# A spectral filter feeding a SiLU layer: table order, stand-ins and the places of weight rounding

## The chip, the cores and the metric

One core of a Trainium2 chip runs the kernel. The metric is the device time of one execution in microseconds (us); the median of several runs counts. Engines are called by their usual names: TensorE (PE) multiplies, PEld is its weight load, VectorE (DVE) and ScalarE (ACT) work element by element, GpSimd (POOL) does the same more slowly, and SyncE (SP) only issues transfers. An engine works through its instructions in order. ScalarE, SyncE and GpSimd also issue transfers (DMA); these rows carry a q, as in SPq.

## The reference

A Fourier filter along the sequence, then a two-layer product with SiLU between, all in float32:

```python
batch, seq, dim = 8, 3008, 256
X = np.fft.rfft(x, axis=1)
Y = X * (filt_r + 1j * filt_i)[None]
y = np.fft.irfft(Y, n=seq, axis=1).astype(np.float32)
x = y.reshape(24064, 256)
h = x @ w_in                          # 256 x 2048
g = h * (1.0 / (1.0 + np.exp(-h)))
out = (g @ w_out).astype(np.float32)  # 2048 x 256
```

## The kernel before

**Two jobs woven together.** The sequence length is 94 x 32. For each batch the spectral part does a first transform over 94 (tiles `pa`), stores and reloads, a second transform over 32 (`pb`), multiplies by the filter, does the two inverse transforms (`pc`, then `pd`, with a store to `d2` and a reload between) and evicts the result as `y`. The layer part takes pairs of 256 tokens from `y` and runs eight steps for a pair, one for each pair of 128-wide slices of the hidden dimension. Products of 2 x 2 blocks are formed from seven products instead of eight: a step has seven products into `px` and `pyz` in `hidden(step)` (L981) and the seven products of the step before into four accumulators in `project` (L1049). Before them, `tokens(pair)` forms the token combinations `ty`, and `combine_weights(jp)` forms the four weight combinations.

**Step and round.** A step is issued in eight rounds. In round 0 stands the first product into `px` and its copy (L989); in round 1 the product into `zo` (half of `pyz`) and its sum `g0`, then `finish()` (two subtractions for the step before); in round 2 the second product into `px` and its copy (L996); in round 3 a product into `yo`; in round 4 the third product into `px`, its copy (L1002) and the second sum of `pyz`; in round 6 the last product into `px`, which a silu then reads; in round 7 the last product into `yo`, whose sum `g1` is the last reader of `pyz`. `px` and `pyz` have one buffer each, so that the next step's products wait for these readers. `pending` is a list, sorted by step and round, of everything else that is to be issued; `put(step, rnd, piece, ...)` adds to it and `until(time)` issues what is due. The order of steps starts with three steps of pair 0, then eight of pair 1, then the rest of pair 0. Slices j = 2 jp and 2 jp + 1 of the weights must be ready when a step first uses jp: steps 0 to 2 use jp 0 to 2, and steps 3 to 10 use jp 0 to 7.

**Weights.** The weights arrive in 64 bits a number, and the kernel makes 32-bit numbers of them with integer and float operations: `load_weights(j)` loads a slice (512 KB), then `bits` (two operations on VectorE, L1179 and L1181), `converted` (two on ScalarE, L1188 and L1189), `added` (VectorE, L1195), `signed` (VectorE, L1200), `placed` (VectorE, L1207). `rounded` is `added` and `signed` in one call. A combination is four operations on VectorE (L952, w_t<-w_t).

**The start.** Batch 0 has nothing to hide behind, and its spectral part runs first, in the same places of `w_t` that the weights take later. `idle(n)` runs n products of no use on TensorE (stand-ins). `load_first` loads x in four parts of 768 KB; `stage1_first(j)` multiplies part j by the table wx3 (48 product records for two parts, since a float32 product is recorded twice) into four banks, and VectorE transposes them. Eight banks serve in turn, so part 2 reuses the banks of part 0. After the second transform of the first groups (`forward`, with twelve stand-ins ahead of group 0) come products, `inverse_first`, and `rows_first`, whose stores to `d2` go out on ScalarE's queue, the last two of the second halves on SyncE's. `load_t4_rows(k)` reloads the rows of groups 2k and 2k+1 (two transfers); `stage3(g)` is the last inverse transform of batch 0's first half. Weights 0 to 5 are begun before the steps. In steps 1 to 6, `stage1(u)` of batch 1 adds two products of 512 columns (L418) in round 3.

In the lists below, `(7, 1, (rounded, 12), ...)` means step 7, round 1.

Of the kernel before, what the change touches and what calls it, by code (L numbers as in the profile page):

```python
# [264 lines left out]
def kernel(  # L265
# [9 lines left out]
    nc = tc.nc  # L275
# [42 lines left out]
    wx_t = cpool.tile([96, 128], FP32)  # L318
# [24 lines left out]
    def bank(b, name, spare=None):  # L343


        if early[0] is None and spare in ("x", "yz"):
            return xps.tile([128, 2, C], FP32, name=name, tag=spare)
        if early[0] is None and spare is not None:
            return accps.tile([128, 2, C], FP32, name=name, tag=f"a{spare}")
        if early[0] is None:  # L350
            return fps.tile([128, 2, C], FP32, name=name, tag="f")
        early[0] += 1
        k = early[0] % 8
        if k < 2:
            return fps.tile([128, 2, C], FP32, name=name, tag="f")
        if k > 5:
            return xps.tile([128, 2, C], FP32, name=name, tag="x" if k == 6 else "yz")
        return accps.tile([128, 2, C], FP32, name=name, tag=f"a{k - 2}")

    def spectral(b):  # L360
# [21 lines left out]
            us["t4"] = view[:, 8960:13056].rearrange("p (n c) -> p n c", c=C)  # L382
            return view

        def stage1_first(j, fill=0):

            raw = [bank(b, f"pa_{b}_{j}_{q}") for q in range(4)]
            ps = [r.rearrange("p a c -> p (a c)").rearrange("p (n c) -> p n c", c=16) for r in raw]
            for _ in range(fill):
                nc.tensor.matmul(out=raw[0][:, 0, 0:128], lhsT=wx_t, rhs=wx_t, start=True, stop=True)  # L390
            for k in range(3):
                for q in range(4):
                    rows = slice(32 * q, 32 * q + 32)
                    nc.tensor.matmul(out=ps[q], lhsT=wx3_t[rows, k], rhs=xs[j][rows, k],  # L394
                                     start=(k == 0), stop=(k == 2), skip_group_check=True)
# [816 lines left out]
    def combine_weights(jp, part=None, eng=None):  # L1212

        eng = eng or v

        def w(c):
            first, by = {A12: (2, 3), S3: (4, -1)}.get(c, (2 * c, 1))
            return flat_w[:, jp, first:first + 2 * by:by]
        if part != 1:
            combine(eng, w(S1), w(S3), w(A22), ALU.add)  # L1220
            combine(eng, w(S2), w(S1), w(A11), ALU.subtract)
        if part != 0:
            combine(eng, w(S3), w(A11), w(S3), ALU.subtract)
            combine(eng, w(S4), w(A12), w(S2), ALU.subtract)
# [6 lines left out]
    def bits(*js):  # L1231
        if wide:
            bits_of_weights(*js)
# [22 lines left out]
    def placed(*js):  # L1256
# [4 lines left out]
                load_exact(j)  # L1261


    nc.scalar.dma_start(out=wx_t, in_=wx_dram.ap())
    wx3_t = qpool.tile([128, 2, C], FP32, name="wx3", tag="q").rearrange("p a c -> p (a c)")[:, 0:384].rearrange(
        "p (k m) -> p k m", k=3)
    nc.scalar.dma_start(out=wx3_t, in_=wx3_dram.ap())
    for i, value in enumerate((1151.0, 255.0 * (1 << 23))):
        nc.gpsimd.memset(bias_t[:, i:i + 1], value)
    for j in range(4):  # L1270
        for i in range(2):
            nc.gpsimd.memset(bias_t[32 * j:32 * j + 32, 3 + i:4 + i], 1.0 if j % 2 == i else -1.0)

    def idle(n, operand=None):

        ps = bank(0, "idle").rearrange("p a c -> p (a c)")
        rows = wx_t if operand is None else operand
        for _ in range(n):
            nc.tensor.matmul(out=ps[:, 0:128], lhsT=rows, rhs=rows, start=True, stop=True)

# [7 lines left out]
    wide_rows = d_t[0:96].rearrange("p s r n -> p (s r n)")[:, 0:256]  # L1288
    blank = x_all[0:96, 0, 0, 0:128]
    v.memset(blank, 0.0)  # L1290
    idle(14, operand=blank)

    part, second = spectral(0), spectral(1)
    part["load_first"]()
    nc.sync.dma_start(out=d_t[:, 0:16], in_=d_dram[:, 0:16])
    nc.sync.dma_start(out=f_all[:, :, 0:4], in_=filt_a)
    nc.sync.dma_start(out=e_t[:, 0:2], in_=e_dram[:, 0:2])
# [12 lines left out]
                                 scale=bias_t[:, 3:4])  # L1310

    for j in range(4):
        part["stage1_first"](j, 5 * (j > 1))
    second["load_two"]()
    weights(4, 5)
    part["forward"](0, fill=12)
# [26 lines left out]
    for k in range(2):  # L1343
        part["add"](NG - 1, k)
    part["load_t4_rows"](0)
    bits(0, 1)
    inverse(4)
    inverse(5)
    converted(0, 1)
    added(0, 1)  # L1350
    part["load_t4_rows"](1)
    part["load_t4_rows"](2)
    bits(2, 3)
    converted(2, 3)
# [4 lines left out]
    combine_weights(0)  # L1359
    rounded(2, 3)  # L1360
    placed(2, 3)
    combine_weights(1)
    bits(4, 5)
    converted(4, 5)
    added(4, 5)
    idle(20)
    for g in range(4):
        part["stage3"](g)
    gp.tensor_copy(out=gate, in_=y[0, 0][:, 0, 28:29])
# [14 lines left out]
    for b in range(1, B):  # L1384
        plan(b, second if b == 1 else spectral(b))
    for step, rnd, *todo in (
            (0, 1, (signed, 4), (placed, 4), (signed, 5)), (0, 5, (placed, 5), (bits, 6), (added, 6)),
            (1, 0, (converted, 6), (weights, 8, 9, 10)), (1, 1, (combine_weights, 2)), (1, 5, (signed, 6), (placed, 6)),
            (2, 1, (bits, 7), (added, 7)), (2, 2, (converted, 7), (weights, 11)),
            (2, 5, (bits, 8), (signed, 7), (placed, 7)), (3, 0, (converted, 8)),  # L1390
            (3, 1, (added, 8), (signed, 8), (placed, 8)), (3, 2, (weights, 12)), (3, 5, (bits, 9), (added, 9)),
            (4, 0, (converted, 9)), (4, 1, (bits, 10), (signed, 9), (placed, 9)),
            (4, 2, (converted, 10), (weights, 13)), (4, 5, (added, 10), (signed, 10), (placed, 10)),
            (5, 1, (combine_weights, 3), (bits, 11)), (5, 2, (converted, 11), (weights, 14, 15)),
            (5, 5, (added, 11), (signed, 11), (placed, 11)),
            (6, 1, (combine_weights, 4), (bits, 12)), (6, 2, (converted, 12)),
            (6, 5, (added, 12), (signed, 12), (placed, 12)),
            (7, 1, (combine_weights, 5), (bits, 13)), (7, 2, (converted, 13)),
            (7, 5, (added, 13), (signed, 13), (placed, 13)),
            (8, 1, (combine_weights, 6), (bits, 14)), (8, 2, (converted, 14)),  # L1400
            (8, 5, (added, 14), (signed, 14), (placed, 14), (bits, 15)), (9, 0, (converted, 15)),
            (9, 1, (added, 15), (signed, 15), (placed, 15)), (9, 5, (combine_weights, 7))):
        for piece, *args in todo:
            put(step, rnd, piece, *args)

# [78 lines left out]
```

## Time and profile before

| | us |
|---|---|
| median of 3 runs | 2517.6 |
| runs | 2517.13, 2517.6, 2519.85 |
| the profiled execution | 2519.81 |
| its span in the profile | 2518.0 |

| engine | busy us | share of the span |
|---|---|---|
| PE | 2491.2 | 99% |
| PEld | 2128.8 | 85% |
| DVE | 1759.4 | 70% |
| ACT | 1096.6 | 44% |
| POOL | 431.5 | 17% |

Times in the profile count from the start of the span. A row of the timeline has start, duration, engine, line, operation, tiles written and read, shapes and count; in brackets stands how long the engine was idle before it and what ended that. A row of the windows has the window, its length, then the busy time and number of instructions of PE, PEld, DVE, ACT and POOL, the granted clock of TensorE (1.00 is full), the share of time that the transfer engines were busy, and GB/s. A row of the waits has engine and line, what it waited for, the sum, how often, and the longest. A row of groups has the count, then busy us, mean ns of one, and idle time before. The line numbers are those of the kernel before; the changed kernel's differ by up to 5 from L388 on (its L392 is L394 here, its L979 is L981).

### The profile page before, as it was taken

The page shows a single profiled execution, that of the slowest core. Times are in us where ns is not written, and L with a number is a line of the kernel's source. Part 1 is how long each engine was busy: PE and PEld are TensorE (multiplying, and loading weights), DVE is VectorE, ACT ScalarE, POOL GpSimd, SP SyncE. Part 2 cuts the span into 40 slices and gives each one's busy share as a digit, 9 for nine tenths or more (in the row PEclk, how much of TensorE's full clock was granted, in tenths as well). Part 3 has the DMA queues.
Part 4 walks back from the last instruction along what each step waited for, and adds up shares of the span by engine and source line. Part 5 has one row for each costly group of instructions (what it writes and reads, how often), then busy time and mean ns, then how long its engine had stood idle before and what let it go on. Part 6 is the DMA issues. An engine that isn't in the chain of part 4 may idle for free.

```text
span 2518.0 us, 42288 instructions
## 1 busy us (share of the span) xinstructions
PE 2491.2 (99%) x16242; PEld 2128.8 (85%) x16242; DVE 1759.4 (70%) x3608; ACT 1096.6 (44%) x3006; POOL 431.5 (17%) x673
## 2 busy tenths in 40 slices
PE   9899999999999999999999999999999999999999
PEld 6678888888888888888888888888888888888988
DVE  6766677777777777777777777777677766655544
ACT  2544444444444444444444444444444444444443
POOL 2201221122121121211222111211122112101100
PEclk9999999999999999999999999999999999999999
DMA  7532141312322132320324203331042211200000
GB/s 268 168 77 88 54 119 46 93 51 58 81 68 72 49 80 60 88 76 25 93 49 117 62 23 79 82 78 43 26 102 66 55 43 34 63 21 9 17 9 17
DMA packets 140089, 170.67 MB, mean 68 GB/s; under 512 B 20892, under 2 KB 113404, under 8 KB 139260
## 3 DMA queue, kind: packets, MB, share of 16 engines
q1 hardware_dynamic: 115824, 120.77, 18.3%
q0 software_dynamic: 22080, 44.10, 6.8%
q8 instruction: 127, 2.08, 0.3%
q10 hardware_dynamic: 1984, 3.11, 0.3%
q14 instruction: 74, 0.61, 0.1%
HBM read 96.06 MB, written 81.26 MB: 70 GB/s over the span
## 4 chain that ended last, share of the span: by engine, by line
PE 96%; DVE 3%; ACT 1%; DMA 0%; issue 0%; POOL 0%; DVEq 0%
PE acc L1049 45%; PE px L981 25%; PE pyz L981 19%; PE pd L756 1%; PE pf L488 1%; PE pc L584 1%; PE pb L546 1%; DVE g L952 1%; PE pa L394 1%; PE pc L662 0%; PE pb L528 0%; PE pa L418 0%; DVE w_t L1207 0%; DMA wx<-wx_tbl 0%; DVE w_t L952 0%
## 5 line engine op out<-in xcount | busy, mean ns | idle before, releaser
L1049 PE MATMUL acc<-g,w_t 128*128 128x256 f32 (+1 forms) x5376 | 1507.7, 376 | 3.0 <-ACT o L769 2.5
L1049 PEld LDWEIGHTS acc<-g,w_t 128*128 128x128 f32 x5376 | 1016.1, 190 | 154.4 <-ACT o L769 15.3
L952 DVE TENSOR_TENSOR g<-pyz,abc 128x256 f32<-128x256 f32 (+1 forms) x1152 | 479.7, 416 | 483.7 <-ACT abc L1002 246.8
L952 DVE TENSOR_TENSOR g<-g 128x256 f32<-128x256 f32 (+3 forms) x1152 | 590.7, 513 | 196.8 <-ACT g L985 183.6
L981 PE MATMUL px<-ty,w_t 128*128 128x256 f32 (+1 forms) x2304 | 676.5, 375 | 5.8 <-ACT abc L1002 5.8
L985 ACT ACTIVATE g<-g 128x256 f32<-128x256 f32 (+1 forms) x1152 | 473.0, 411 | 246.0 <-DVE g L952 246.0
L981 PEld LDWEIGHTS px<-ty,w_t 128*128 128x128 f32 x2304 | 434.1, 190 | 63.8 <-ACT abc L1002 7.8
L952 POOL TENSOR_TENSOR s<-s 128x256 f32<-128x256 f32 (+1 forms) x322 | 246.8, 784 | 1389.1 <-DVE s L1075 1046.6
L981 PE MATMUL pyz<-y,w_t 128*128 128x256 f32 (+1 forms) x1536 | 452.7, 376 | 6.8 <-DVE g L952 6.6
L981 PEld LDWEIGHTS pyz<-y,w_t 128*128 128x128 f32 x1536 | 282.7, 189 | 53.8 <-DVE g L952 14.5
L996 ACT COPY abc<-px 128x256 f32<-128x256 f32 (+1 forms) x384 | 141.6, 369 | 370.6 <-PE px L981 370.6
L985 ACT ACTIVATE g<-px 128x256 f32<-128x256 f32 (+1 forms) x384 | 146.1, 381 | 302.4 <-PE px L981 302.4
L1002 ACT COPY abc<-px 128x256 f32<-128x256 f32 (+1 forms) x384 | 141.7, 369 | 306.2 <-PE px L981 306.1
L981 PE MATMUL px<-y,w_t 128*128 128x256 f32 (+1 forms) x768 | 227.5, 378 | 0.9 <-ACT y L734 0.9
L981 PE MATMUL pyz<-ty,w_t 128*128 128x256 f32 (+1 forms) x768 | 225.7, 376 | 0.0
L981 PEld LDWEIGHTS px<-y,w_t 128*128 128x128 f32 x768 | 143.9, 190 | 22.9 <-DVE q L777 1.9
L981 PEld LDWEIGHTS pyz<-ty,w_t 128*128 128x128 f32 x768 | 142.4, 190 | 20.8 <-DVE g L952 0.5
L989 ACT COPY abc<-px 128x256 f32<-128x256 f32 (+1 forms) x384 | 135.5, 353 | 35.0 <-PE px L981 35.0
L508 POOL DMA_DIRECT2D d<-tf x96 | 48.8, 508 | 215.7 <-DVE tf L438 210.5
L1075 ACT COPY s<-acc 128x512 f32<-128x512 f32 (+1 forms) x92 | 53.1, 578 | 46.2 <-issue 27.8
L605 POOL DMA_DIRECT2D d<-low x36 | 22.3, 620 | 286.0 <-DVE low L601 286.0
L478 DVE TENSOR_TENSOR uf<-x_all 120x512 f32<-120x512 f32 (+1 forms) x72 | 60.2, 864 | 0.3 <-issue 0.3
(129 smaller groups left out, 1364.1 us busy)
## 6 DMA issues: line engine op xcount, KB each, us to landing
t<-d SPq DMA_DIRECT2D x84, 256.0 KB
t<-d SPq DMA_DIRECT2D x224, 96.0 KB
out_dram<-s SPq DMA_DIRECT2D x62, 256.0 KB
d<-q POOLq DMA_DIRECT2D x48, 256.0 KB, 5.3
x_all<-in_x_dram SPq DMA_DIRECT2D x96, 96.0 KB
x_all<-xr SPq DMA_DIRECT2D x96, 96.0 KB
d<-tf POOLq DMA_DIRECT2D x96, 96.0 KB, 2.7
d<-tq POOLq DMA_DIRECT2D x96, 96.0 KB, 2.8
```

The lines of the kernel that those rows point to most:

```text
L394: nc.tensor.matmul(out=ps[q], lhsT=wx3_t[rows, k], rhs=xs[j][rows, k], start=(k == 0), stop=(k == 2), skip_group_check=True)
L478: nc.vector.tensor_tensor(out=out, in0=in0, in1=in1, op=op)
L488: nc.tensor.matmul(out=ps[q][32 * k:32 * k + 32], lhsT=wq_t[rows, k], rhs=rhs[k][rows], start=True, stop=True)
L508: nc.gpsimd.dma_start(out=d1[par, :, grp, at:at + 4], in_=part[rows].rearrange("p q n c -> p (q n) c"))
L952: eng.tensor_tensor(out=out, in0=in0, in1=in1, op=op)
L981: nc.tensor.matmul(out=out, lhsT=w_t[:, jp, c, 0], rhs=rhs, start=start, stop=True, skip_group_check=True)
L985: nc.scalar.activation(out=g[:, k, 0:n], in_=g[:, k, 0:n] if src is None else src, func=AFT.Silu)
L989: nc.scalar.copy(out=sums[:, 0, 0:n], in_=xo)
L996: nc.scalar.copy(out=sums[:, 1, 0:n], in_=xo)
L1002: nc.scalar.copy(out=sums[:, 2, 0:n], in_=xo)
L1049: nc.tensor.matmul(out=acc[pair][i][:, h, 0:n], lhsT=w_t[:, jp, OUT_PLACE.get(c, c), 1], rhs=g[:, k, 0:n], start=(new and h == 0), stop=la ...
L1075: copy(out=dst, in_=src)
```

## The change

- The table `wx3` is loaded first on SyncE's queue, ahead of x, and `wx_t` behind x; both were on ScalarE's queue.
- The first stand-ins are 12 instead of 14. The five stand-ins ahead of parts 2 and 3 of the first transform are gone.
- The reload of the middle rows (groups 2 and 3) is issued on GpSimd's queue, right behind the reload of the first rows.
- The stand-ins ahead of `stage3` are twenty of 32 x 32 and eleven of 128 columns instead of twenty of 128 columns.
- `combine_weights(1)`, `bits`, `converted` and `added` of weights 4 and 5 move from ahead of `stage3` into steps 0 and 1.
- The pieces of weights 4 to 15 get new places in steps 0 to 9: conversions stand at rounds 0 and 5, combinations at round 5 (of the step ahead of their use), `added`, `signed` and `placed` mostly at round 1, and some `bits` at round 7. Some loads of weights come later.
- `tokens(1)` moves from step 1, round 5 to step 2, round 1, and `tokens(2)` from step 12 to step 11, round 5.

The number and sizes of all useful operations stay the same, and so does the order of TensorE's useful products.

```diff
-        def stage1_first(j, fill=0):
+        def stage1_first(j):
...
-            for _ in range(fill):
-                nc.tensor.matmul(out=raw[0][:, 0, 0:128], lhsT=wx_t, rhs=wx_t, start=True, stop=True)
...
-    nc.scalar.dma_start(out=wx_t, in_=wx_dram.ap())
...
-    nc.scalar.dma_start(out=wx3_t, in_=wx3_dram.ap())
+    nc.sync.dma_start(out=wx3_t, in_=wx3_dram.ap())
...
-    def idle(n, operand=None):
+    def idle(n, operand=None, small=0):
...
+        for _ in range(small):
+            nc.tensor.matmul(out=ps[0:32, 0:32], lhsT=wx_t[0:32, 0:32], rhs=wx_t[0:32, 0:32], start=True, stop=True)
...
-    idle(14, operand=blank)
+    idle(12, operand=blank)
...
     part["load_first"]()
+    nc.sync.dma_start(out=wx_t, in_=wx_dram.ap())
...
-        part["stage1_first"](j, 5 * (j > 1))
+        part["stage1_first"](j)
...
     part["load_t4_rows"](0)
+    part["load_t4_rows"](1, nc.gpsimd)
     bits(0, 1)
...
-    part["load_t4_rows"](1)
     part["load_t4_rows"](2)
...
     placed(2, 3)
-    combine_weights(1)
-    bits(4, 5)
-    converted(4, 5)
-    added(4, 5)
-    idle(20)
+    idle(11, small=20)
...
-            (0, 1, (signed, 4), (placed, 4), (signed, 5)), (0, 5, (placed, 5), (bits, 6), (added, 6)),
-            (1, 0, (converted, 6), (weights, 8, 9, 10)), (1, 1, (combine_weights, 2)), (1, 5, (signed, 6), (placed, 6)),
-            (2, 1, (bits, 7), (added, 7)), (2, 2, (converted, 7), (weights, 11)),
-            (2, 5, (bits, 8), (signed, 7), (placed, 7)), (3, 0, (converted, 8)),
-            (3, 1, (added, 8), (signed, 8), (placed, 8)), (3, 2, (weights, 12)), (3, 5, (bits, 9), (added, 9)),
-            (4, 0, (converted, 9)), (4, 1, (bits, 10), (signed, 9), (placed, 9)),
-            (4, 2, (converted, 10), (weights, 13)), (4, 5, (added, 10), (signed, 10), (placed, 10)),
-            (5, 1, (combine_weights, 3), (bits, 11)), (5, 2, (converted, 11), (weights, 14, 15)),
-            (5, 5, (added, 11), (signed, 11), (placed, 11)),
-            (6, 1, (combine_weights, 4), (bits, 12)), (6, 2, (converted, 12)),
-            (6, 5, (added, 12), (signed, 12), (placed, 12)),
-            (7, 1, (combine_weights, 5), (bits, 13)), (7, 2, (converted, 13)),
-            (7, 5, (added, 13), (signed, 13), (placed, 13)),
-            (8, 1, (combine_weights, 6), (bits, 14)), (8, 2, (converted, 14)),
-            (8, 5, (added, 14), (signed, 14), (placed, 14), (bits, 15)), (9, 0, (converted, 15)),
-            (9, 1, (added, 15), (signed, 15), (placed, 15)), (9, 5, (combine_weights, 7))):
+            (0, 1, (combine_weights, 1), (bits, 4)), (0, 5, (converted, 4), (bits, 5), (added, 4)),
+            (1, 0, (converted, 5), (weights, 8, 9, 10)), (1, 1, (signed, 4), (placed, 4), (rounded, 5), (placed, 5)),
+            (1, 5, (combine_weights, 2)),
+            (2, 1, (bits, 6), (added, 6)), (2, 5, (converted, 6), (bits, 7)), (3, 0, (converted, 7)),
+            (3, 1, (signed, 6), (placed, 6), (added, 7)), (3, 5, (signed, 7), (placed, 7)), (3, 7, (bits, 8)),
+            (4, 0, (converted, 8), (weights, 11)), (4, 1, (rounded, 8), (placed, 8), (bits, 9)), (4, 2, (weights, 12)),
+            (4, 5, (converted, 9), (added, 9), (bits, 10)), (5, 0, (converted, 10), (weights, 13)),
+            (5, 1, (signed, 9), (placed, 9), (rounded, 10), (placed, 10)),
+            (5, 5, (combine_weights, 3)), (5, 7, (bits, 11)), (6, 0, (converted, 11), (weights, 14, 15)),
+            (6, 1, (rounded, 11), (placed, 11), (bits, 12)), (6, 5, (converted, 12), (combine_weights, 4)),
+            (6, 7, (bits, 13)), (7, 0, (converted, 13)),
+            (7, 1, (rounded, 12), (placed, 12), (rounded, 13)), (7, 5, (combine_weights, 5)), (7, 7, (bits, 14)),
+            (8, 0, (converted, 14)), (8, 1, (placed, 13), (rounded, 14), (placed, 14), (bits, 15)),
+            (8, 5, (converted, 15), (combine_weights, 6)),
+            (9, 1, (rounded, 15), (placed, 15)), (9, 5, (combine_weights, 7))):
...
-        step, rnd = combines[pair % per] if pair not in (1, 2) else ((1, 5), (12, 5))[pair - 1]
+        step, rnd = combines[pair % per] if pair not in (1, 2) else ((2, 1), (11, 5))[pair - 1]
```

More of the change, by code (lines that the diff above doesn't have):

```diff
@@ L383, in load_first @@
             return view
-        def stage1_first(j, fill=0):
-            raw = [bank(b, f"pa_{b}_{j}_{q}") for q in range(4)]
-            ps = [r.rearrange("p a c -> p (a c)").rearrange("p (n c) -> p n c", c=16) for r in raw]
-            for _ in range(fill):
-                nc.tensor.matmul(out=raw[0][:, 0, 0:128], lhsT=wx_t, rhs=wx_t, start=True, stop=True)
+        def stage1_first(j):
+            ps = [bank(b, f"pa_{b}_{j}_{q}").rearrange("p a c -> p (a c)").rearrange(
+                "p (n c) -> p n c", c=16) for q in range(4)]
             for k in range(3):
```

## The prediction

> **What bounds the kernel now.** I read the page first, then TensorE's own rows of the first 66 us, its waits, the chain, and last the order of each engine's instructions in both kernels. All edits lie in the first 175 us of
>
> ```profile
> span 2518.0 us, 42288 instructions
> ```
>
> and TensorE is what ends late there: from 1 us on it runs almost without a pause, so a microsecond counts only where TensorE stands idle, repeats stand-ins, or runs slowly.
>
> ```profile
> 1.08 6.34 PE L1279 MATMUL idle<-x_all 96*128 96x128 f32 x28 [1.08 <-DVE x_all L1290]
> 8.67 8.37 PE L394 MATMUL pa<-w_t,wx 32*128 32x512 f32 x48 [1.25 <-DMA wx<-wx_tbl]
> 16.97 1.38 PE L390 MATMUL pa<-wx_t 96*128 96x128 f32 x10
> 18.29 2.86 PE L394 MATMUL pa<-w_t,wx 32*128 32x512 f32 x24
> 21.07 1.38 PE L390 MATMUL pa<-wx_t 96*128 96x128 f32 x10
> 22.38 2.86 PE L394 MATMUL pa<-w_t,wx 32*128 32x512 f32 x24
> 25.17 2.94 PE L521 MATMUL pb<-d_t,wx_t 96*128 96x128 f32 x24
> 28.05 2.30 PE L528 MATMUL pb<-w_t,d_t 64*32 64x256 f32 x72
> ```
>
> These are TensorE's rows up to the second transform. To see are the wait for the table wx before the first real products, two groups of ten stand-ins between quarters (L390), and that 48 products take 8.37 where twice 24 would take 5.72: the first ones run at about half speed. The second stretch is the end of the first transform:
>
> ```profile
> 51.29 4.63 PE L1279 MATMUL idle<-wx_t 96*128 96x128 f32 x40
> 56.14 0.29 PE L720 MATMUL pd<-wi_t,w_t 64*64 64x47 f32 x2 [0.22 <-DMA w_t<-d]
> 57.16 2.09 PE L720 MATMUL pd<-wi_t,w_t 64*64 64x47 f32 x123 [0.73 <-DMA w_t<-d]
> 60.70 2.13 PE L720 MATMUL pd<-wi_t,w_t 64*64 64x47 f32 x128 [1.45 <-issue]
> 64.15 0.32 PE L720 MATMUL pd<-wi_t,w_t 64*64 64x47 f32 x3 [1.32 <-issue]
> 64.40 0.70 PE L1285 MATMUL idle<-d_t,wx_t 96*128 96x256 f32 x2
> 65.96 0.79 PE L981 MATMUL px<-y,w_t 128*128 128x256 f32 x1 [0.86 <-ACT y L734]
> ```
>
> From 65.96 the steps run. I compare steps 1 to 9 (their first products start at 71.68 and 149.96) with one free step, by windows; the third window holds the clock of step 0 (second figure from the PEclk column):
>
> ```profile
> 71.68:149.96 78.28, 68.29 (x276) 51.41 (x277) 58.85 (x132) 42.29 (x98) 12.08 (x24) 1.00 0.47 138
> 180.69:186.73 6.04, 6.04 (x29) 5.32 (x28) 4.50 (x10) 2.40 (x7) 0.00 (x0) 1.00 0.49 123
> 66.00:72.00 6.00, 5.52 (x15) 3.34 (x16) 5.31 (x11) 2.12 (x6) 3.61 (x8) 0.73 1.00 327
> ```
>
> Nine free steps would take 9 x 6.04 = 54.4; steps 1 to 6 also carry the next batch's first transform, 1.72 each by the chain (10.3):
>
> ```profile
> 110.55 1.72 PE pa L418 x4
> ```
>
> So 78.28 - 64.7 = 13.6 us of these steps is loss. TensorE's waits between 66 and 180 us name its causes: ScalarE's third copy of px behind the conversions of weights, and VectorE's sums behind their rounding; the rest is each interrupted product run draining.
>
> ```profile
> PE px L981 <- ACT abc L1002: 5.8, 5, 1.7
> PE pyz L981 <- DVE g L952: 5.5, 10, 1.1
> ```
>
> **Table first on the load queue.** The chain begins with the table's transfer, on ScalarE's queue beside the quarters of x on SyncE's:
>
> ```profile
> 1.29 7.24 DMA wx<-wx_tbl
> ...
> 40.21 7.67 PE pc L662 x128
> ```
>
> It lands at 8.53. SyncE's first issue that had to wait for the first quarter of x is
>
> ```profile
> 5.34 0.34 SPq L1297 DMA_DIRECT2D e_t<-e_tbl  x1
> ```
>
> so that quarter (768 KB) was in at 5.3. With the 192 KB table ahead of it, a quarter of its size, I put it at 5.9 (estimate from the same row). The stand-ins before it shrink from 14 to 12: 6.34 x 12/14 = 5.43, from 1.08 to 6.5. So the first products start at 6.5, bound by the stand-ins, against 8.67: 2.15 us. Later loads carry the same bytes; wx_t, now behind x, is first read in the twelve stand-ins before the second transform, far later. If the quarter came late instead, up to 1 us of this goes.
>
> **No stand-ins between quarters.** Each L390 group costs 1.3 (16.97 to 18.29). Quarter 2 reuses the banks of quarter 0, which VectorE transposes while quarter 1 is multiplied, so nothing waits where they stood: 2.6 us for both. If transposes or data were late, part comes back as wait; bounds 0 and 2.6. The slow first products stay slow for about as long as now, which is in both kernels. By then the second transform starts 4.8 us earlier, at 23.3, and the chain behind it (products, inverse, stores, reloads) is made by compute and moves with it.
>
> **Middle rows on GpSimd's queue, other stand-ins at 51 us.** The reload that ends last is the third; it cannot be issued before the last stores have landed, so moving the middle one away frees nothing that ends the stretch: 0. Its cover: GpSimd is idle then, but its queue's 256 KB transfers are slow,
>
> ```profile
> d<-q POOLq DMA_DIRECT2D x48, 256.0 KB, 5.3
> ```
>
> 5.3 us from issue to landing; the last reload needs about as long after its stores, so I bound this between a gain of 0.5 and a loss of 1. Stand-ins: eleven large ones cost 11/20 of 4.63 = 2.5. Twenty small ones are not in the trace: at the spacing of the small products (2.13/128 each, two per stand-in) 0.7, at the price of large ones 4.6. The cover runs to 57.16 less 51.29 = 5.9; their sum is 3.2 to 7.1, I take 4.5, being nearer to the small products' row in shape: 0, with 1.2 to lose. The two stops of 1.45 and 1.32 have no cause in the trace; the count of instructions ahead changes by one product, so I leave them.
>
> **Weights 4 and 5 leave the front.** ScalarE's six evictions of y stand behind the conversions of 4 and 5:
>
> ```profile
> 63.58 2.32 ACT L734 COPY y<-pd 128x376 f32<-128x376 f32 x6
> ...
> 64.51 0.55 DVE L734 COPY y<-pd 128x376 f32<-128x376 f32 x1 [1.05 <-PE pd L720]
> ```
>
> Without them four of the six are done before the last products, and y is ready with VectorE's copy at 65.06, when the 0.70 filler also ends: the 0.86 wait goes. But step 0 now holds combine_weights(1) and bits 4 ahead of the second sum, and the conversion of 4 ahead of the silu of px, which releases px for step 1. I take 0.4 back (0 to 0.8). Net 0.5.
>
> **New places in steps 0 to 9.** What VectorE has free in a step shows in one that carries no weights:
>
> ```profile
> 157.83 0.42 DVE L952 TENSOR_TENSOR g<-pyz,abc 128x256 f32<-128x256 f32 x1 [1.33 <-PE pyz L981]
> ...
> 162.17 0.42 DVE L952 TENSOR_TENSOR g<-pyz,abc 128x256 f32<-128x256 f32 x1 [1.62 <-ACT abc L1002]
> ```
>
> 1.33 at round 5 (before the sum that frees pyz for the next step) and 1.62 at round 1, which the transform's 1.72 widens to 3.3 in steps 1 to 6. The pieces cost
>
> ```profile
> L1189 ACT ACTIVATE e<-e,bias_t 128x512 uint32<-128x512 f32 x10 | 7.2, 722 | 0.3
> L1207 DVE SCALAR_TENSOR_TENSOR w_t<-m,e 128x512 f32<-128x512 f32 x10 | 6.9, 692 | 0.3
> ...
> L1181 DVE TENSOR_SCALAR m<-raw 128x512 uint32<-128x512 uint32 x10 | 4.2, 422 | 0.0
> ```
>
> 0.69 for each of add, sign and place (0.64 where they follow one another), 0.8 for bits, 1.45 for a conversion (two such), and a combine
>
> ```profile
> 149.10 1.55 DVE L952 TENSOR_TENSOR w_t<-w_t 128x256 f32<-128x256 f32 x4
> ```
>
> which already stands at round 5 of step 9 and is followed by no listed wait. Old: 1.9 to 2.9 at round 5 (three pieces or more, once with tokens), and conversions at round 2, ahead of the third copy of px. New: at most one combine, or 1.4, at round 5; up to five pieces (3.2) at round 1, which steps 1 to 6 hold (3.3); conversions at round 0 or 5. What is late next, by step:
> - 2, 4, 6: the conversion at round 5 stands before the silu that frees px: 0 to 1.45 each, taken 0.35, since TensorE still has two products to run there; 1.05.
> - 3: two drains of the accumulators share round 5 with two pieces: 0.7, as now.
> - 7: no transform widens it; five pieces and the bits put at round 7 of step 6 make 3.2 + 0.8 - 1.6 = 2.4 late at the second sum; the fourth product into pyz follows a little later, so 1.6.
> - 8: the same 2.4, and the conversion of 15 must wait for bits 15, the last of that row, with the silu of px behind it: 0.9; 3.3.
>
> New loss 6.65, so 13.6 - 6.65 = 7.0 gained; bounds 3 (new waits twice as long) and 11.
>
> tokens(2) moves from round 5 of step 12, where two products of the next batch stand too, to step 11, whose end is covered by the transform work that opens step 12. The wait
>
> ```profile
> 174.18 0.70 PE L981 MATMUL pyz<-y,w_t 128*128 128x256 f32 x2 [0.88 <-DVE g L952]
> ```
>
> goes: 0.9.
>
> **Sum.** 2.15 + 2.6 + 0 + 0.5 + 7.0 + 0.9 = 13.1, from the profiled execution's 2519.8 (its span and 1.8 around it): 2506.7. That execution lies 2.2 above the median, 2517.6; the three runs are 2517.1, 2517.6 and 2519.9. I think that part of this spread is when the clock rises and falls, as in the window of 66 to 72, and that a typical run of the changed kernel lies a little below the sum: I forecast 2506.
>
> **Rivals.**
> *The waits return.* Step waits are replaced one for one (13.6 stays, conversions at round 5 cost their full 1.45): only start, y and tokens are gained, 6.1: 2511.5 to 2513. For it: VectorE is busy 58.85 of 78.28 and gets 4.4 more (a combine 1.55, two bits 1.6, two adds 1.3). Against: the transform's slack, used by five steps. 0.17.
> *The start gives little* (x late, transposes late): 2.4 less, 2508.5; 0.10.
> *Nearly all waits go*: 2502; 0.09.
> *Slower: the clock.* The 48 products lost 8.37 - 5.72 = 2.65 to the slow clock, so it lasted some 5.3 us of them, to about 14, although stand-ins ran from 1.08. It also fell in step 0: 0.73 in the window of 66 to 72, after pauses of at most 1.45. If removing stand-ins (2 + 10, and weak small ones) leaves the clock low through the second transform and inverse, those rows cost double: two quarters 5.7, fillers 2.9, transform 2.30 x 128/72 = 4.1, inverse 7.67, 20 in all, less the 13: 2519.8 + 7 = 2527. It decides if the speed is not up when the second transform starts. Against: from 6.5 on TensorE has no pause, and the quarters' products are the very ones under which it rose. 0.04.
> *No change* (moves only trade places under other limits, some mix): 2516; 0.04.
> The Trainium skill (TensorE: Matmul & The Clock Gate, Part 1) says that a free-running window of about 3.4 us of idleness halves the clock and a busy one restores it; by it no removal here could slow anything, and the sum would stand at 2506.7. The trace does not agree: the fall in step 0 came after no pause of that length.
>
> **Numbers.** 0.2% of 2517.6 is 5.0 us, about what a measurement can tell from no change. Forecast 0.56 (2503 to 2510). Faster (below 2512.6): 0.56 + 0.10 + 0.09 and most of the first rival: 0.87; same 0.09; slower 0.04. Range 2501.5 to 2513: from all waits gone with the lower level to the waits' return.
>
> **What would show it.** First real product at 6.5, no L390, second transform at 23 to 24; steps begin near 60; px no longer waits on L1002 at 1.7; steps 1 to 6 near 7.8 each, step 8 the longest; no wait near step 13. Wrong if the first quarters' products wait for DMA, if half-speed rows reach past 18, or if steps 1 to 9 still take over 75.

## The result, and the profile after

The changed kernel takes 2508.6 us (median of 6 runs, 2507.8 to 2509.6) against 2519.3 (6 runs, 2517.1 to 2519.9): a ratio of 0.9959, 95% interval 0.9947 to 0.9972, so 7 to 13 us. The forecast was 2506, within 2501.5 to 2513. The runs of before spread over 2.7 us, so that their median depends on the draw: 2517.6 for the first three, 2519.3 for all six. The profiled execution took 2507.81, 12.0 less than the profiled one of before; that one lies 0.5 above its median and this one 0.8 below its own, which makes the medians' 10.7.

```profile
span 2506.0 us, 42288 instructions
```

TensorE's rows up to the second transform and, below, of the end of the first inverse:

```profile
1.08 5.49 PE L1278 MATMUL idle<-x_all 96*128 96x128 f32 x24 [1.08 <-DVE x_all L1289]
6.50 11.43 PE L392 MATMUL pa<-w_t,wx 32*128 32x512 f32 x96
17.86 2.94 PE L519 MATMUL pb<-d_t,wx_t 96*128 96x128 f32 x24
20.73 3.65 PE L526 MATMUL pb<-w_t,d_t 64*32 64x256 f32 x117
```

```profile
45.14 1.45 PE L1276 MATMUL idle<-wx_t 32*32 32x32 f32 x40
46.52 2.72 PE L1278 MATMUL idle<-wx_t 96*128 96x128 f32 x22
51.36 0.29 PE L718 MATMUL pd<-wi_t,w_t 64*64 64x47 f32 x2 [2.12 <-ACT t L421]
52.31 5.53 PE L718 MATMUL pd<-wi_t,w_t 64*64 64x47 f32 x252 [0.66 <-DMA w_t<-d]
59.15 0.26 PE L718 MATMUL pd<-wi_t,w_t 64*64 64x47 f32 x2 [1.32 <-issue]
...
60.15 0.67 PE L979 MATMUL px<-y,w_t 128*128 128x256 f32 x2
```

The first real products start at 6.50, with no wait, and nothing stands between the quarters. The second transform starts at 20.73 instead of 28.05: 7.3 us sooner, where 4.8 were forecast. But step 0 starts at 60.15 instead of 65.96, only 5.8 sooner: ahead of the products pd stand a pause of 2.12 and one of 0.66, and 252 of them take 5.53 where the kernel before ran 251 in 2.09 + 2.13, with a stop of 1.45 between.

Steps 1 to 9 by windows (the first row; the columns are span of the window, TensorE, its weight loads, VectorE, ScalarE, GpSimd, granted clock, DMA share, GB/s), then step 11 and the window in which the clock was low:

```profile
65.68:137.43 71.75, 68.45 (x276) 51.15 (x277) 62.44 (x138) 43.87 (x100) 11.86 (x24) 1.00 0.52 157
...
144.92:155.59 10.67, 9.67 (x129) 7.53 (x128) 7.42 (x14) 4.31 (x12) 4.73 (x6) 1.00 0.02 5
52.08:55.49 3.41, 3.18 (x120) 3.21 (x123) 2.11 (x4) 0.85 (x2) 0.00 (x0) 0.50 0.02 5
```

71.75 against 78.28: 6.53 gained. TensorE's waits between 60 and 170 us:

```profile
PE pyz L979 <- DVE g L950: 3.0, 8, 0.8
PE pd L718 <- DVE g L950: 1.0, 1, 1.0
PE px L979 <- ACT g L983: 0.8, 2, 0.4
PE px L979 <- ACT abc L1000: 0.5, 1, 0.5
```

The wait of px for ScalarE's third copy, five times and up to 1.7 before, stands once, with 0.5; VectorE's sums still hold pyz (3.0 instead of 5.5), and one wait is new, of a transform product pd.

By the starts of the steps, the 12.0 us of the two profiles lie as follows: 5.81 at step 0, 0.19 in step 0, 6.53 in steps 1 to 9, 0.02 in steps 10 to 13, and 0.55 lost in small steps from step 14 to the end.

### The profile page after: what moved, and what is told of

The parts are those of the page before. It is cut to its first block, busy times and chain, and to the rows that moved or that the text cites. A ratio compares the mean times of both kernels' runs of the same rounds, so it can differ in the third digit from the quotient of the medians.

```text
span 2506.0 us, 42288 instructions
## 1 busy us (share of the span) xinstructions
PE 2485.5 (99%) x16240; PEld 2126.6 (85%) x16240; DVE 1758.7 (70%) x3608; ACT 1097.1 (44%) x3006; POOL 433.3 (17%) x675
## 4 chain that ended last, share of the span: by engine, by line
PE 97%; DVE 2%; ACT 0%; DMA 0%; issue 0%; POOL 0%; SPq 0%; DVEq 0%; ACTq 0%
PE acc L1047 45%; PE px L979 26%; PE pyz L979 19%; PE pd L754 1%; PE pf L486 1%; PE pc L582 1%; PE pb L544 1%; DVE g L950 0%; PE pa L392 0%; PE pc L660 0%; PE pa L416 0%; PE pd L718 0%; PE pb L526 0%; DMA w_t<-d 0%; PE pc L640 0%
```

## The experiments

Each run is compared with the kernel before on the same chip in the same set. The kernel before took 2518.1 in the set of "the new places", "the table", "more stand-ins" and "tokens(2) elsewhere"; 2519.6 in that of "no stand-ins", "the pause", "middle rows" and "a better version"; 2517.7 in that of the last three. Between sets only the ratios compare. A profile is one execution. Where the text says "the stretch", it means the time from the second transform's start to step 0: 37.91 before, 39.42 after.

**The new places alone** (before, with the step list and tokens(1) of the change):

```diff
-    combine_weights(1)
-    bits(4, 5)
-    converted(4, 5)
-    added(4, 5)
     idle(20)
...
-            (0, 1, (signed, 4), (placed, 4), (signed, 5)), (0, 5, (placed, 5), (bits, 6), (added, 6)),
+            (0, 1, (combine_weights, 1), (bits, 4)), (0, 5, (converted, 4), (bits, 5), (added, 4)),
...
-        step, rnd = combines[pair % per] if pair not in (1, 2) else ((1, 5), (12, 5))[pair - 1]
+        step, rnd = combines[pair % per] if pair not in (1, 2) else ((2, 1), (12, 5))[pair - 1]
```

> The kernel before with one part of the change alone: the new places of the weight rounding in steps 0 to 9 (weights 4 and 5 leave the front, tokens(1) goes to round 1 of step 2); start, stand-ins, middle rows and tokens(2) as before. Theory, from the two traces: the steps' gain belongs to the list itself, so y no longer waits (step 0 starts about 0.9 us earlier, near 65.1) and steps 1 to 9 take 71.7 instead of 78.28: about 7.4 us less than the kernel before, some 2512. Rival: part of that gain came from the full clock in step 0 and the earlier start; then steps 1 to 9 stay above 74 here and the time is near 2515.

2510.8, ratio 0.9966 (0.9955 to 0.9978). Steps 1 to 9 take 71.77, the same as in the changed kernel:

```profile
70.81:142.58 71.77, 68.47 (x276) 51.26 (x277) 62.50 (x138) 43.82 (x100) 12.04 (x24) 1.00 0.51 153
```

So the list makes the steps' 6.5 by itself; the rival falls. Step 0 started at 64.59, 1.37 sooner than before, but the second transform had started 1.22 sooner too (26.83), with the same code ahead of it. That pointed at the clock. Of the 0.86 that y's wait was to give, 0.15 came (stretch 37.76): pd now waited 1.16 for its rows.

**The table alone** (before, with wx first on SyncE's queue, wx_t behind x, 12 stand-ins):

```diff
-    nc.scalar.dma_start(out=wx_t, in_=wx_dram.ap())
-    nc.scalar.dma_start(out=wx3_t, in_=wx3_dram.ap())
+    nc.sync.dma_start(out=wx3_t, in_=wx3_dram.ap())
-    idle(14, operand=blank)
+    idle(12, operand=blank)
     part["load_first"]()
+    nc.sync.dma_start(out=wx_t, in_=wx_dram.ap())
```

> The kernel before with the table wx leading the load queue, wx_t behind x and 12 instead of 14 stand-ins; the groups of stand-ins between quarters stay. Theory (clock): in the kernel before, the 1.25 us wait for wx broke the stretch of work under which the clock would have risen, so that it rose at 14.6; with no wait it rises at 7.7, and the second transform starts at about 23.5 instead of 28.05, 4.6 us earlier of which 2.15 are the earlier start; time about 2514.7. Rival (the prediction): the slow first products last as long as before, the second transform starts at 25.9, time about 2517.2.

2515.0, ratio 0.9988 (0.9979 to 0.9998). The first 48 products take 6.00 instead of 8.37, and the second transform starts at 23.50, as the clock theory said:

```profile
6.50 6.00 PE L394 MATMUL pa<-w_t,wx 32*128 32x512 f32 x48
...
23.50 3.87 PE L528 MATMUL pb<-w_t,d_t 64*32 64x256 f32 x128
```

Of these 4.55 us 3.95 are left at step 0, where y now waits for ScalarE's conversions of 4 and 5.

**More stand-ins instead of the wait** (before):

```diff
-    idle(14, operand=blank)
+    idle(19, operand=blank)
```

> The kernel before with 19 instead of 14 stand-ins ahead of the first products, so that TensorE has no pause while it waits for wx (still on its old queue, in at 8.5). Theory (clock): the clock rises near 7.8, the stand-ins after that run at double speed and end near 8.8, the 96 products take 11.4 beside the stand-ins between quarters, and the second transform starts near 26.0 although the first product starts no earlier. Rival (the clock rises after a fixed amount of real products, or at a fixed time): 19 stand-ins end at 9.7, the first products stay slow and the second transform starts near 29.0, the time is 1 us longer than before.

2517.3, ratio 0.9995 (0.9986 to 1.0005): no verdict on the time. The pause wasn't removed, since the clock had risen during the stand-ins (at 5.08) and they ended early, yet the 48 products run at full speed:

```profile
1.08 6.40 PE L1279 MATMUL idle<-x_all 96*128 96x128 f32 x38 [1.08 <-DVE x_all L1290]
8.63 5.43 PE L394 MATMUL pa<-w_t,wx 32*128 32x512 f32 x48 [1.16 <-DMA wx<-wx_tbl]
```

The rival (it takes real products, or a fixed time) falls. That a pause of 1.16 always keeps the clock low falls too; what decides is where the pause lies in the clock's windows (last section). In the profile step 0 starts at 63.00, 2.96 sooner than in that of before, but the medians differ by 0.8 only. This suggests that the profiled execution of before lost more to the clock than a typical one.

**No stand-ins between quarters** (before):

```diff
-        part["stage1_first"](j, 5 * (j > 1))
+        part["stage1_first"](j)
```

> The kernel before without the two groups of stand-ins between the quarters of the first transform, nothing else. Prediction's term: 2.6 us, second transform at 25.4 instead of 28.05 (or 24.2 where the clock happens to rise a little sooner, as in one run of the same start). Theory: the products in place of the stand-ins run at the clock that they find, so the 2.6 come in full at the second transform, but about 0.8 of it is lost again ahead of step 0, where the reload of the rows becomes late. Rival: the transposes of the first quarters are late and part returns as waits inside the first transform.

2515.4, ratio 0.9987 (0.9977 to 0.9996). The 96 products run without a gap, so no transpose is late:

```profile
8.61 12.51 PE L394 MATMUL pa<-w_t,wx 32*128 32x512 f32 x96 [2.20 <-DMA wx<-wx_tbl]
...
23.92 3.88 PE L528 MATMUL pb<-w_t,d_t 64*32 64x256 f32 x128
```

Of 4.13 gained at the second transform, 2.6 are the groups and the rest is the clock, which rose sooner than in the profile of before. All 4.13 stand at step 0, so the expected loss of 0.8 did not come (stretch 37.90).

**tokens(2) elsewhere** (the changed kernel):

```diff
-        step, rnd = combines[pair % per] if pair not in (1, 2) else ((2, 1), (11, 5))[pair - 1]
+        step, rnd = combines[pair % per] if pair not in (1, 2) else ((2, 1), (12, 1))[pair - 1]
```

> The changed kernel with tokens(2) at round 1 of step 12 instead of round 5 of step 11. In the changed kernel step 11 takes 10.67 (9.37 in the kernel before) and step 13 takes 7.27 (8.41 before), so that the move gave -0.16 where 0.9 was forecast. Theory: at round 5 of step 11 the sums of tokens hold up the sum that frees pyz, in whose bank the transform work that opens step 12 is multiplied; at round 1 of step 12, where VectorE has 1.6 us free, step 11 falls to 9.4 or less, step 12 stays below 5.7 and step 13 stays near 7.3: 1.0 to 1.3 us less than the changed kernel. Rival: the 1.55 us of sums only move the wait to step 12 (5.28 becomes 6.5 or more): no gain.

2508.0, ratio 0.9957 (0.9942 to 0.9972), which doesn't tell it from the changed kernel, but the steps do: 11 to 13 take 9.36, 5.29 and 7.37, against 10.67, 5.28 and 7.27.

```profile
145.65:155.01 9.36, 9.36 (x129) 7.35 (x127) 5.32 (x11) 4.31 (x12) 3.50 (x5) 1.00 0.03 6
155.01:160.30 5.29, 5.29 (x33) 4.61 (x26) 3.96 (x9) 2.10 (x6) 1.97 (x3) 1.00 0.89 220
160.30:167.67 7.37, 7.37 (x61) 5.66 (x60) 4.89 (x11) 2.44 (x8) 0.00 (x0) 1.00 0.11 38
```

1.2 us gained, and no pause of TensorE in the three. In the changed kernel the sums of tokens(2) stand ahead of the sum that frees pyz, and the products pd of the transform work wait 1.00 for that bank.

**The pause before pd filled** (the changed kernel):

```diff
-    idle(11, small=20)
+    idle(20, small=20)
```

> The changed kernel with twenty large stand-ins instead of eleven behind the twenty small ones, so that TensorE has nothing idle where it stood 2.12 us before the inverse products pd (51.36 in the changed kernel). The wait itself, for t copies on ScalarE, stays. Theory: that pause made the clock fall (half speed 52.08 to 55.49), so that the 252 products pd took 5.53 where the kernel before needs about 4.3; with the pause filled the clock stays, the products take 4.3 to 4.6, and step 0 starts about 1 us sooner after the second transform's start (39.4 in the changed kernel, 38.4 here). Rival: the products are held by the loading of their instructions (a 1.3 to 1.5 us stop) and by the third reload, whatever the clock; 39.4 stays, or the stand-ins overrun and it grows.

2506.9, ratio 0.9949 (0.9934 to 0.9964). The clock stays up, and the products take 3.77 and 0.56 with one stop:

```profile
46.67 4.73 PE L1278 MATMUL idle<-wx_t 96*128 96x128 f32 x40
51.33 0.32 PE L718 MATMUL pd<-wi_t,w_t 64*64 64x47 f32 x2
52.68 3.77 PE L718 MATMUL pd<-wi_t,w_t 64*64 64x47 f32 x234 [1.04 <-DMA w_t<-d]
57.42 0.56 PE L718 MATMUL pd<-wi_t,w_t 64*64 64x47 f32 x20 [0.98 <-issue]
```

From the rows' arrival to step 0 it takes 6.04 (52.68 to 58.72), in the changed kernel 7.84 (52.31 to 60.15). The products go at 16.1 ns each (3.77 for 234) instead of 21.9 (5.53 for 252), so in this pair the slow clock cost the products 252 x 5.8 ns = 1.5 us; the other 0.3 is a shorter stop. The stops vary, though. In a later run (first row loads on GpSimd's queue, below) the clock fell in the same place and 254 products took 5.63, but no stop stood among them, and from the rows to step 0 it took 6.36, only 0.3 more than here. By these profiles the fall costs between 0.3 and 1.8 us in all, and which of them is typical isn't settled; the ratios of this run and of the changed kernel overlap. The rival is right that a stop and the wait for the rows stay. It is wrong that the clock makes no difference to the products; for the total this stays open. The rest of the stretch's shortening (to 36.76, where 38.4 was expected) is that the transform started 1.2 later here while the rows arrived nearly at the same time: in this profile the row loads are the next bound.

**Middle rows on the load queue** (the changed kernel):

```diff
-    part["load_t4_rows"](1, nc.gpsimd)
...
+    part["load_t4_rows"](1)
     part["load_t4_rows"](2)
```

> The changed kernel with the middle row loads back on the load queue, ahead of the third ones; all else as in the changed kernel. The prediction priced the move to the other queue at 0 (between a gain of 0.5 and a loss of 1): pd's wait for the rows at 52.07 would stay within 0.3 us, since the third row loads end last in both. Rival: the third row loads are then issued behind the middle ones, whose issue itself waits, and land 1 to 2 us later, so step 0 starts 1 us or more later.

2509.0, ratio 0.9959 (0.9944 to 0.9974). In the profile the main run of pd starts 1.7 us later than in the changed kernel (54.04 for 52.31), and step 0 too; counted from the second transform, which starts 0.16 later here, it is 1.6 (stretch 41.01). The ratios are the same, so the times show no difference.

```profile
53.10 0.41 PE L718 MATMUL pd<-wi_t,w_t 64*64 64x47 f32 x2 [3.94 <-DMA w_t<-d]
54.04 6.30 PE L718 MATMUL pd<-wi_t,w_t 64*64 64x47 f32 x253 [0.53 <-DMA w_t<-d]
```

In this profile the middle row loads go out at 42.76, and the third ones wait not for them, as the rival had it, but for ScalarE's last store. That store goes out at 43.84 in both kernels and lands after 5.63 here (the third ones start at 49.49), after 3.30 in the changed kernel (47.16). Stores of this size took between 3.3 and 5.7 with the middle rows on GpSimd's queue too (below). So the 1.6 of this profile, though above the forecast's upper bound of 0.5, isn't shown to come from the queue.

**A better version** (the changed kernel with three edits):

```diff
-    idle(11, small=20)
+    idle(20, small=20)
-            (3, 1, (signed, 6), (placed, 6), (added, 7)), (3, 5, (signed, 7), (placed, 7)), (3, 7, (bits, 8)),
+            (3, 1, (signed, 6), (placed, 6), (rounded, 7), (bits, 8)), (3, 5, (placed, 7)),
-        step, rnd = combines[pair % per] if pair not in (1, 2) else ((2, 1), (11, 5))[pair - 1]
+        step, rnd = combines[pair % per] if pair not in (1, 2) else ((2, 1), (12, 1))[pair - 1]
```

> The changed kernel with three edits: tokens(2) at round 1 of step 12, twenty large stand-ins ahead of pd, and in step 3 the rounding of weight 7 and bits 8 at round 1 (only the placing of 7 stays at round 5). In the changed kernel step 4 takes 9.19, with a wait of 0.54 for the sum that stands behind two drains and two pieces of weight 7, and one of 0.19 behind bits 8; VectorE has 1.56 us free at round 1 of step 3. Theory: step 4 falls to about 8.3 with step 3 still below 8.2, step 11 is 9.4, step 13 is 7.3 to 7.4: some 2 to 3 us less than the changed kernel, 2505.5 to 2507. Rival: step 3 grows by what step 4 loses, and the time is that of the run with tokens(2) at step 12 alone, 2508.

2504.3, ratio 0.9941 (0.9924 to 0.9957); its four runs (2504.0 to 2504.7) lie below all six of the changed kernel, though those are of another set and the intervals of the two ratios overlap. Step 3 keeps its 7.87 and step 4 falls from 9.19 to 8.02:

```profile
79.98:87.85 7.87, 7.87 (x33) 6.16 (x33) 6.97 (x14) 6.01 (x14) 2.07 (x6) 1.00 0.35 97
87.85:95.87 8.02, 8.01 (x34) 5.80 (x33) 6.82 (x16) 5.79 (x14) 2.14 (x5) 1.00 0.76 233
```

The rest of the 3.9 between the two profiles is the 1.2 of tokens(2) and the 1.5 sooner start of step 0.

**What makes the rows late: three more runs on the better version.** The chain of waits of the changed kernel between 38 and 61 us, in order of time:

```profile
39.59 4.17 DMA w_t<-d
...
43.84 3.30 DMA d<-q
...
47.75 4.32 DMA w_t<-d
...
52.31 5.53 PE pd L718 x249
```

ScalarE's last store of q was ready at 42.5 and went out at 43.84, behind the landing of the first of these row loads at 43.77. In the trace the two signal the same semaphore (number 101), one of eight that the transfers take in turn. In the kernel before they share it too, but there that row load had landed at 46.65, ahead of the copy, and the store went out with its copy at 48.51. First, those row loads on GpSimd's queue:

```diff
-    part["load_t4_rows"](0)
+    part["load_t4_rows"](0, nc.gpsimd)
```

> The better version with the first row loads of the reload on GpSimd's queue too, ahead of the middle ones. In the better version ScalarE's last store of q is ready at 41.9 and is issued at 43.11 only, behind a wait for the landing of these first row loads (43.03), and the third row loads wait for that store and land at 52.41, which sets the start of pd. Theory: off the load queue the store no longer waits for them, is issued near 42, the third loads land near 51.3, and step 0 starts about 1 us sooner (37.87 from the start of the second transform in the better version, 36.9 here). Rival: the wait is on the rows whichever queue carries them, and the slower queue lands them later: the store is issued at 44 or later and step 0 starts 1 us later.

2504.9, ratio 0.9948 (0.9934 to 0.9963). The store goes out with its copy, at 42.41, as expected; but now the store on SyncE's queue lands late and holds the third rows:

```profile
42.59 5.68 DMA d<-q
...
49.00 4.60 DMA w_t<-d
```

```profile
53.73 5.63 PE L718 MATMUL pd<-wi_t,w_t 64*64 64x47 f32 x254 [1.04 <-DMA w_t<-d]
```

pd starts at 53.73, and nothing is gained: one wait in the place of another. The pauses of 1.00 and 1.04 ahead of pd fell into one window of the clock, which was 0.50 from 54.52 to 57.94, in spite of the twenty large stand-ins; the products took 5.63, this time without a stop.

Second, the loads of weights 4 and 5 moved from ahead of the second transform to behind the third row loads:

```diff
-    weights(4, 5)
     part["forward"](0, fill=12)
...
     part["load_t4_rows"](2)
+    weights(4, 5)
```

> The better version with the loads of weights 4 and 5 issued behind the third row loads instead of ahead of the second transform (their bits are first taken in step 0). In the better version two of ScalarE's stores of q wait for landings of weight loads (until 35.97 and 37.87), so that the first row loads start at 39.34. Theory: these waits go, the first row loads are issued some 1 us sooner, ScalarE's last store is no longer held at 43.0, the third row loads land near 51.2, and step 0 starts about 1 us sooner (36.9 from the start of the second transform instead of 37.87). Rival: the stores' landings, 3.9 us each, set the chain in any case, and the late weights share the load queue with the third rows: no gain, or up to 1 us lost.

2503.5, ratio 0.9944 (0.9929 to 0.9958). Both waits of the stores go and pd starts 10.4 us after the last copy of q (40.64 to 51.03), in the better version 10.5 (42.15 to 52.65). The profile's chain names a late weight load as what pd waited for:

```profile
40.66 3.86 DMA d<-q
...
45.85 5.15 DMA raw<-in_moe_w_dram
...
51.03 3.77 PE pd L718 x234
```

In the trace, though, that load is not wholly in before 51.83, after pd has begun. The third rows are in at 50.79, 0.24 ahead of pd, as far as in the changed kernel (52.07 and 52.31). The later of their two transfers took 5.6 from its issue (45.20) beside the weight loads, and 3.8 in the better version. This fits the rival; one profile doesn't show that sharing the queue was the cause.

Third, both edits together:

> Both of the last two edits on the better version. Theory: the waits of ScalarE's stores, for weight loads and for the first rows, are all that made the third row loads late against the products; without both, the last store goes out with its copy (near 41.9 for a second transform at 20.75), the third rows land near 50.5 to 51, the 20 large stand-ins (end 50.9) become the bound, and step 0 starts 1.3 to 1.5 us sooner than in the better version: about 2503. Rival: one of the edits alone gives all of it, or GpSimd's queue becomes the late one: 2504 or more.

2504.4, ratio 0.9949 (0.9932 to 0.9966). Rows in at 51.34, stretch 37.53 against 37.87, not the 1.3 to 1.5 expected. From the last copy of q to pd the three take 11.2, 10.4 and 10.8 us, the better version 10.5: whatever wait was removed ahead of it, the last store and the reload behind it took as long. None of the three is told from the better version by its median.

## Why the prediction was right or wrong

The direction held, and 2508.6 lies in the range, 2.6 above the forecast. By the two profiles 12.0 us came of the 13.1 summed, but two large errors of opposite sign stand behind that, so that the sum came this near in part by luck. The step from 2506.7 to 2506 took the profiled execution of before to lie 2.2 above its median; with six runs it lies 0.5 above, so this step had no ground. Point by point:

*Start, 2.15 forecast.* 2.17 came (8.67 to 6.50), bound by the stand-ins as said.

*No stand-ins between quarters, 2.6.* It came in full; no transpose or data was late.

*"The slow first products stay slow for about as long as now".* This step failed, and it brought more than forecast. The wait for wx had not only cost its 1.25 us. It lay in the stretch of work that would have raised the clock: before, the clock rose at 14.64, after it at 7.70. In all nine profiles in which TensorE has no pause there, it rose between 6.1 and 10.7, and the second transform of the eight with the changed start began at 20.0 to 22.2, not at the forecast's 23.3. Worth 2.6 us in this pair, 1.1 to 3.3 over these runs.

*"The chain behind it is made by compute and moves with it".* This failed too, and took that gain back. With y's wait gone, step 0 was to start 0.86 sooner after the second transform; it started 1.51 later. From that start to the last copy of q: 21.77 instead of 20.62, with a new stop of 0.97 before an inverse product that the profile puts to issue. Such a stop (0.71 to 0.97) stands in three of the eight profiles with the changed start; the other five take 20.6, so this part differs from run to run. From there to pd: 9.8 instead of 8.5, since stores and reloads, not products, now set the end. This part is in all eight profiles (9.8 to 11.8; in the five with the old front 8.5 to 9.0). From pd to step 0: 7.84 instead of 8.80. The chain of the kernel before ran elsewhere in this place, through VectorE's rounding and ScalarE's conversions up to y:

```profile
56.46 1.21 DVE raw L1200 x2
57.66 1.21 DVE w_t L1207 x2
...
63.67 2.24 ACT y L734 x6
```

The prediction shows two earlier rows of this chain and not this part. Its sum puts nothing down for reloads that end later than the work in front of them; before, pd waited for them 0.22 and 0.73.

*Stand-ins at 51, at 0 with 1.2 to lose.* Their length was estimated well (4.5; measured 1.45 + 2.72), but pd now starts 7.2 after their beginning, not 5.9. The pause left let the clock fall for 3.4 us, which cost the products 1.5 in this profile. With it filled, pd to step 0 takes 6.04 instead of 8.80: 0.86 of that is y's wait, as forecast with weights 4 and 5 gone from the front, and 1.8 is that one stop of 0.98 stands where two made 1.45 + 1.32. The prediction left these two stops as they were.

*Step 0, 0.4 given back.* It took 5.53 instead of 5.72, but the kernel before ran it partly at the low clock. The run with the new places alone had the low clock there too (64.28 to 67.69) and took 6.22: at a like clock about 0.5 was given back, as forecast, and the full clock hid it.

*Middle rows, 0 (from -1 to 0.5 gained).* 1.6 in the one profile without the move; the times cannot tell. The reason given held: with the middle loads on either queue, the third ones went out when the last store had landed. What differed was how long that store took, 3.30 or 5.63.

*Steps 1 to 9, 7.0 (6.65 left as loss).* 6.53 gained, 7.05 left, and the run with the list alone gave the same 71.77. By step the terms hold within 0.6 (step 7 7.58, forecast 7.64; step 8 8.88, forecast 9.3), except step 4: 9.19, forecast 8.1. The 0.7 for two drains was put on step 3 and came as a wait of 0.54 at the first sum of step 4; the bits put at round 7 of step 3 stand there too, and were not priced. The statement that step 8 would be the longest was wrong for that reason.

*tokens(2), 0.9.* Nothing came: steps 10 to 13 together gained 0.02. "Covered by the transform work that opens step 12" was the error: that work is multiplied in the banks of px and pyz, so it waits for the very sum that stands behind tokens(2). At round 1 of step 12 the move gives 1.2 in the profile.

**The rivals.** "The start gives little" gave 2508.5, very near the result, but by late data and late transposes, and neither came; the loss lay behind the second transform. The rival of a clock that stays low found the right mechanism in the wrong place: the clock fell, but at pd, where stand-ins had been cut, and for one window. "The waits return" is excluded by the 71.75 of steps 1 to 9, "nearly all waits go" by the 7.05 left there, and "no change" by the ratio.

**The rule that the prediction set aside.** The Trainium skill (TensorE: Matmul & The Clock Gate, Part 1) counts busy and idle in free-running windows of about 3.4 us. The prediction set this aside because the clock had fallen after no pause of that length. The traces agree with the windows, whose phase changes from run to run (3.41 us, last section), and the rule would have given the sooner rise, at 7.70 behind a window of work. They do not agree that a whole window must be idle: the clock fell after windows with as little as 1.38 us idle.

## What to carry to other kernels

Follow the chain of waits through the whole stretch that an edit shortens: work that is moved up stops at the first transfer that does not move with it, and cover sized for the old start is then too short. A short wait early in a kernel can cost more than its length through the clock (here 1.25 us of wait, and 2.6 us more in this pair of profiles), and a pause left by cutting stand-ins can let the clock fall too. Before work is moved ahead of the last reader of a PSUM bank, look for who else uses that bank.

## What the hardware showed that was not expected

**The clock goes by windows of 3.41 us.** Low-clock stretches in the traces last 3.41 or 6.83 us (the start and the last 30 us left out), and rises and falls of one run lie on one grid whose phase differs between runs. The rows below have the window, its length, TensorE's busy time and products, the granted clock, DMA share and GB/s. In the kernel before, 12 products stand in the window that holds most of the wait for wx, 20 in the first full one, and then 33 at full speed:

```profile
7.81:11.23 3.42, 2.56 (x12) 1.00 1.01 418
11.23:14.64 3.41, 3.41 (x20) 1.00 1.02 407
14.64:18.05 3.41, 3.41 (x33) 1.00 1.05 428
```

and in the changed one (the clock column shows 1.00 where the trace has no record yet; the counts tell the speed):

```profile
0.88:4.29 3.41, 3.21 (x15) 1.00 0.75 231
4.29:7.70 3.41, 3.41 (x19) 1.00 1.00 396
7.70:11.12 3.42, 3.42 (x40) 1.00 1.01 413
48.66:52.08 3.42, 0.87 (x8) 1.00 0.62 152
52.08:55.49 3.41, 3.18 (x120) 0.50 0.02 5
```

Over the 13 profiles, ahead of the last 30 us, the clock fell after twelve windows with 1.38 to 3.22 us idle, and stayed up after windows with up to 1.72. Between 1.38 and 1.72 both happened, above that it always fell: about half a window idle was enough. It rose after windows with at most 0.46 idle, and in 22 of 25 cases at most 0.02. In four profiles a first window without any idle time left it low, and only the second raised it; why is open.

**Stores and reloads that came sooner took longer.** From the last copy of q to pd, with the same bytes, it took 8.5 to 9.0 us in the five profiles in which that copy ends at 44.5 to 48.7, and 9.8 to 11.8 in the eight in which it ends at 40.6 to 42.9; a 256 KB store on this path took 3.3 to 5.7 us to land. What slows them wasn't settled: the eight are the changed kernel and its variants, which differ in more than the time. Nor was the cause found of TensorE's stops of 0.4 to 1.6 us ("issue") among the short products pd, which stand in 12 of the 13 profiles, nor that of the 0.55 us lost from step 14 on.
